# Layer A with keys-by-queries scores and a bounded exponential behind a runtime branch, and layer B's projections resident

## The chip, the cores and the metric

The kernel runs on one core of one Trainium2 chip. The metric is the device time of one execution in microseconds (us), median of several. The four executions of the kernel before lie within 0.24% (3440.38 to 3448.54). "Fast" is the label that the record gives to a run.

Five engines matter: PE (matrix products; PEld is its weight load), DVE (vector), ACT (scalar functions), POOL (general purpose) and SP (used here to issue DMA transfers). In the traces each has its own timeline, and for a wait the profile names what ended it, as in "PE b_tail <- DMA b_wq: 17.4 us" further down.

## The reference, cut to what matters

Four layers, A B A B, over 2048 tokens of width 640. Layer A has 32 heads of width 20. It works in four segments of 512 tokens. In each it computes causal softmax attention and, from the second segment on, a linear "memory" read; the two are mixed by a gate per head. phi(t) is t + 1 above 0 and exp(t) below. Layer B walks 64 steps in sequence (32 tokens plus 8 memory tokens each).

```python
x = x + _A_ref(_layernorm(x), A_wq, A_wk, A_wv, A_wo, A_beta)
x = x + _B_ref(_layernorm(x), B_mem0, B_Wq, B_Wk, B_Wv, B_Wo, B_seg_len)
# ... both once more

# inside _A_ref, for each of the 4 segments s:
logits = einsum('bhqd,bhkd->bhqk', qs, ks) * scale + mask   # mask: -1e9 above the diagonal
p      = softmax(logits);  a_dot = einsum('bhqk,bhkd->bhqd', p, vs)
a_mem  = einsum('bhld,bhde->bhle', phi(qs), M) / (phi(qs) . z + 1e-6)
o      = g * a_mem + (1 - g) * a_dot
M, z   = M + phi(ks)^T vs, z + sum(phi(ks))
```

The weights are drawn small. The product that the new kernel's bound tests is an estimated 0.0025 against a limit of 0.075, so these inputs take the bounded branch.

## The kernel before: the parts that the change touches

Layer A, one head of one segment (256 of these in the two layers), queries on the partitions:

```python
def S_stage(u):                       # scores, row maximum, exponential
    for qc in range(4):
        N = 128 * (qc + 1)
        nc.tensor.matmul(Sx[:, 0:N], lhsT=stt["qTm"][:, j, 128*qc:128*qc+128], rhs=kT[:, 0:N], ...)
        nc.tensor.matmul(Sx[:, N-128:N], lhsT=C.identb[:], rhs=C.negu[:], ...)      # causal mask, on PE
        nc.vector.tensor_reduce(out=negm[:], in_=Sx[:, 0:N], op=ALU.max, negate=True)
        nc.scalar.activation(out=Pj[:, OFFS[qc]:OFFS[qc]+N], in_=Sx[:, 0:N], func=ACT.Exp, bias=negm[:, 0:1])
def T_stage(u):                       # P has queries on partitions: transpose it for the value product
    for bi in range(8):
        nc.tensor.transpose(tpA[:, bi, :], Pj[...], C.identb[:])
    # ... 2 more into tpB; tpA and tpB copied to PTj by DVE and ACT
def PV_stage(u):
    nc.tensor.matmul(PVu[:, qc, :], lhsT=PTj[:, bidx, :], rhs=va[:, kc, j, :], ...)
```

The layer norm of the next segment is applied by DVE (`layernorm_tile`). The padded weights of A are built anew in each A layer, and all four weights of B (5.2 MB each) are loaded at each start of B:

```python
def load_B_weights(...):
    for nm, src in (("wq", B_Wq), ("wk", B_Wk), ("wv", B_Wv)):
        nc.sync.dma_start(t[:], src.rearrange("(c p) h e -> p c (h e)", p=128))
    nc.sync.dma_start(W.wo[:], B_Wo.rearrange("h e d -> e h d"))
```

## Time and profile before

| | us |
|---|---|
| median of 3 runs | 3443.7 (3440.38 to 3448.54) |
| span of the profiled run | 3445.3 |
| start, until the first score of A | 39.7 |
| A loop, first / second | 437.9 / 446.1 |
| tail of A (last score to last output projection) | 17.5 / 17.4 |
| joint (from there to the first step of B) | 61.5 / 62.6 |
| B and the second start of A | 1196.6 |
| second B | 1166.0 |

All such rows in this document are differences between the starts of first or last matmuls as the trace's tile view lists them (`a_S` scores, `a_YP` output projection, `b_Qa` first projection of a step of B), so that every kernel is cut at the same places.

The costliest groups of layer A (tiles: `a_S` scores, `a_negm` row maxima, `a_Pj` exponentials, `a_tpA` transposes), from the page of the kernel before (line, engine, operation, output<-input, shape, count, then busy us, mean ns of one, and what the idle time before it waited for):

```profile
L338 ACT ACTIVATE a_Pj<-a_S,a_negm 128x128 bf16<-128x128 f32 (+3 forms) x1024 | 504.0, 541 | 48.8 <-DVE a_negm L337 42.9
L337 DVE TENSOR_REDUCE a_negm<-a_S 128x1 f32<-128x128 f32 (+3 forms) x1024 | 467.7, 482 | 76.9 <-PE a_S L335 48.3
...
L348 PE MATMUL a_tpA<-c_identb,a_Pj 128*128 128x128 bf16 x2048 | 232.4, 220 | 8.0 <-ACT a_Pj L338 2.8
...
L335 PE MATMUL a_S<-c_negu,c_identb 128*128 128x128 bf16 x1024 | 221.3, 219 | 0.0
```

The two A loops in the windows view of the kernel before (stretch in us, its length, busy us of PE, PEld, DVE, ACT and POOL with their numbers of instructions, mean granted PE clock as a fraction of full speed, DMA share, GB/s):

```profile
40.00:478.00 438.00, 389.19 (x4968) 288.74 (x5008) 382.68 (x997) 375.96 (x857) 119.45 (x198) 0.99 0.09 27
1753.00:2199.00 446.00, 398.81 (x4967) 294.51 (x5003) 383.97 (x996) 377.60 (x857) 113.47 (x190) 0.97 0.10 30
```

In the loop PE is busy 389 of 438 us, DVE 383, ACT 376, and POOL only 119. Three engines are busy 86 to 89% of it at once, so the change sets out to relieve all three. At the joint the waits view shows PE waiting for B's weights (what waited, for what, us in all, times, longest):

```profile
PE b_tail L103 <- DMA b_wq<-in_B_Wq_dram: 17.4, 1, 17.4
PE b_tail L103 <- DMA b_wk<-in_B_Wk_dram: 6.1, 1, 6.1
...
PE b_tail L103 <- DMA b_wv<-in_B_Wv_dram: 5.2, 1, 5.2
```

### The profile page before, as it was taken

The page shows a single profiled execution, that of the slowest core. Times are in us where ns is not written, and L with a number is a line of the kernel's source. Part 1 is how long each engine was busy: PE and PEld are TensorE (multiplying, and loading weights), DVE is VectorE, ACT ScalarE, POOL GpSimd, SP SyncE. Part 2 cuts the span into 40 slices and gives each one's busy share as a digit, 9 for nine tenths or more (in the row PEclk, how much of TensorE's full clock was granted, in tenths as well). Part 3 has the DMA queues.
Part 4 walks back from the last instruction along what each step waited for, and adds up shares of the span by engine and source line. Part 5 has one row for each costly group of instructions (what it writes and reads, how often), then busy time and mean ns, then how long its engine had stood idle before and what let it go on. Part 6 is the DMA issues. An engine that isn't in the chain of part 4 may idle for free. (4 is left out here: it accounts for less than half of the span.)

```text
span 3445.3 us, 130756 instructions
## 1 busy us (share of the span) xinstructions
PE 3017.7 (88%) x56899; PEld 1780.5 (52%) x56980; DVE 2075.8 (60%) x5369; ACT 1691.9 (49%) x3987; POOL 660.2 (19%) x1687
## 2 busy tenths in 40 slices
PE   5988867999999999999769888679999999999998
PEld 4666643555454554555446666435555555554554
DVE  7888863555555555555488888625555555555554
ACT  5978852343333433334269788523443334333332
POOL 4242220111111111111132322201111111111111
PEclk9999987999999999999889999879999999999998
DMA  2010034000000000000120111340000000000000
GB/s 66 13 40 26 22 136 174 17 19 17 20 17 17 19 17 20 17 17 15 24 69 12 48 29 30 143 166 15 17 15 17 15 15 17 15 17 15 15 13 11
DMA packets 94208, 120.95 MB, mean 35 GB/s; under 512 B 31424, under 2 KB 79552, under 8 KB 89792
## 3 DMA queue, kind: packets, MB, share of 16 engines
q1 hardware_dynamic: 93632, 112.58, 10.9%
q8 instruction: 446, 7.31, 0.9%
q14 instruction: 130, 1.06, 0.1%
HBM read 72.13 MB, written 23.59 MB: 28 GB/s over the span
## 5 line engine op out<-in xcount | busy, mean ns | idle before, releaser
L103 PEld LDWEIGHTS <-b_hT 128*32 128x32 bf16 x15520 | 356.2, 96 | 376.9 <-DVE b_hT L103 46.6
L338 ACT ACTIVATE a_Pj<-a_S,a_negm 128x128 bf16<-128x128 f32 (+3 forms) x1024 | 504.0, 541 | 48.8 <-DVE a_negm L337 42.9
L337 DVE TENSOR_REDUCE a_negm<-a_S 128x1 f32<-128x128 f32 (+3 forms) x1024 | 467.7, 482 | 76.9 <-PE a_S L335 48.3
L103 PE MATMUL b_OPS<-b_wo,b_OTsb 128*32 128x320 bf16 x8192 | 318.5, 310 | 44.3 <-DVE b_OTsb L103 44.3
L103 PE MATMUL b_V<-b_wv,b_hT 128*32 128x512 bf16 x5120 | 346.9, 382 | 0.0
L103 POOL TENSOR_TENSOR b_P<-b_Pu,b_rs 128x256 bf16<-128x256 bf16 (+1 forms) x256 | 111.2, 455 | 1181.9 <-DVE b_rs L103 1181.9
L103 ACT ACTIVATE b_Pu<-b_SP 128x320 bf16<-128x320 f32 x256 | 111.9, 437 | 357.3 <-DVE b_SP L103 357.3
L103 PEld LDWEIGHTS <-b_OTsb 128*32 128x32 bf16 x8192 | 213.2, 100 | 118.4 <-DVE b_OTsb L103 57.9
L348 PE MATMUL a_tpA<-c_identb,a_Pj 128*128 128x128 bf16 x2048 | 232.4, 220 | 8.0 <-ACT a_Pj L338 2.8
L103 ACT COPY b_QT<-b_TPQ 128x128 bf16<-128x128 bf16 x508 | 178.3, 379 | 119.7 <-PE b_TPQ L103 115.9
L103 DVE COPY b_KT<-b_TPK 128x128 bf16<-128x128 bf16 x382 | 101.7, 266 | 218.6 <-PE b_TPK L103 218.6
L103 DVE CAST b_hT<-b_MT 128x24 bf16<-128x24 f32 x126 | 23.0, 183 | 330.7 <-PE b_MT L103 330.7
L335 PE MATMUL a_S<-c_negu,c_identb 128*128 128x128 bf16 x1024 | 221.3, 219 | 0.0
L103 ACT CAST b_msb<-b_OPS 128x320 bf16<-128x320 f32 x128 | 54.4, 425 | 296.3 <-PE b_OPS L103 296.3
L103 PE MATMUL b_Qa<-b_wq,b_hT 128*32 128x512 bf16 x2560 | 163.4, 384 | 34.7 <-DVE b_hT L103 34.7
L103 DVE CAST b_Ksb<-b_Ka 128x512 bf16<-128x512 f32 x128 | 88.5, 691 | 149.9 <-PE b_Ka L103 149.6
L103 ACT ACTIVATE b_Qsb<-b_Qb 128x512 bf16<-128x512 f32 x128 | 76.4, 597 | 198.1 <-PE b_Qb L103 198.1
L348 PEld LDWEIGHTS <-a_Pj 128*128 128x128 bf16 x2048 | 147.0, 98 | 50.2 <-issue 10.1
L103 PEld LDWEIGHTS <-b_hx 128*32 128x32 bf16 x3840 | 84.9, 98 | 164.7 <-issue 58.5
L103 DVE TENSOR_REDUCE b_negmax<-b_SP 128x8 f32<-128x320 f32 x256 | 124.8, 487 | 71.1 <-PE b_SP L103 71.1
L103 DVE TENSOR_REDUCE b_ssum<-b_Pu 128x8 f32<-128x320 bf16 x256 | 123.1, 481 | 72.4 <-ACT b_Pu L103 72.4
L103 DVE CAST b_Ksb<-b_Kb 128x512 bf16<-128x512 f32 x128 | 88.5, 691 | 125.9 <-PE b_Kb L103 125.9
(357 smaller groups left out, 6588.1 us busy)
## 6 DMA issues: line engine op xcount, KB each, us to landing
xres<-a_xnew SPq DMA_DIRECT2D x32, 320.0 KB
b_wq<-in_B_Wq_dram SPq DMA_DIRECT2D x2, 5120.0 KB
b_wk<-in_B_Wk_dram SPq DMA_DIRECT2D x2, 5120.0 KB
b_wv<-in_B_Wv_dram SPq DMA_DIRECT2D x2, 5120.0 KB
b_wo<-in_B_Wo_dram SPq DMA_DIRECT2D x2, 5120.0 KB
b_Vt<-b_Vtb SPq DMA_DIRECT2D x512, 16.0 KB
b_XO<-xres SPq DMA_DIRECT2D x256, 30.0 KB
xres_bf<-a_xnb SPq DMA_DIRECT2D x32, 160.0 KB
```

The lines of the kernel that those rows point to most:

```text
L103: r = f(*a, **k)
L335: nc.tensor.matmul(Sx[:, N - 128:N], lhsT=C.identb[:], rhs=C.negu[:], start=False, stop=True)
L337: nc.vector.tensor_reduce(out=negm[:], in_=Sx[:, 0:N], axis=AX.X, op=ALU.max, negate=True)
L338: nc.scalar.activation(out=Pj[:, OFFS[qc]:OFFS[qc] + N], in_=Sx[:, 0:N], func=ACT.Exp, bias=negm[:, 0:1], scale=1.0)
L348: nc.tensor.transpose(tpA[:, bi, :], Pj[:, OFFS[qc] + 128 * kc: OFFS[qc] + 128 * kc + 128], C.identb[:])
```

## The change

The intent: compute the scores with keys on the partitions, so that the exponential already has the layout which the value product needs. The transposes and their copies go away. A softmax without its row maximum is safe if |score| is bounded: the kernel computes a bound from the column norms of the weights at run time and branches. In the bounded branch the mask becomes a select on POOL after the exponential. Four heads of 32 padded rows are packed into PE's row tiles (the trace lists these matmuls as `32*128`, the full array's as `128*128`). B's wq, wk and wv are loaded once, during the first A layer, and stay; only wo is loaded at each B. The layer norm of the next segments moves from DVE to POOL.

The diff, cut to its core (cuts marked; the whole is 834 lines):

```diff
-def load_A_weights(nc, tc, ctx, C, A_wq, A_wk, A_wv, A_wo, A_beta):     # ... per A layer
+def prep_A(nc, tc, C, A_wq, A_wk, A_beta):                              # once
+        for k, src in enumerate((A_wq, A_wk)):
+            nc.gpsimd.memset(pad[:], 0.0)
+            # ... 5 copies into pad (3 DVE, 2 ACT), 8 stores of padded weights to DRAM
+            nc.gpsimd.tensor_tensor(out=sq[:], in0=raw[:], in1=raw[:], op=ALU.mult)
+            nc.vector.tensor_reduce(out=hs[:, k, :], in_=sq[:]..., op=ALU.add)
+        # ... maximum over heads, compared with the limit
+        W.bounded = nc.values_load(flag[0:1, 0:1])
 ...
+            def score(u, r):          # part r of unit u: two heads, one to three key blocks
+                for kc, c0 in ((0, 0),) if part == 0 else ((1, 0),) if part == 1 else ((2, 0), (3, 256)):
+                    for jj in range(2):
+                        nc.tensor.matmul(Sx[:, jj, c0:c0+N], lhsT=U.qk[32*j:32*j+32, 1, 128*kc:128*kc+128],
+                                         rhs=U.qk[32*j:32*j+32, 0, 128*kc:512], tile_position=(32*j, 0))
+                nc.scalar.activation(out=PT[:], in_=Sx[:, :, 0:N], func=ACT.Exp, scale=SC)
+                for c0 in ((0,), (0,), (0, 256))[part]:
+                    nc.gpsimd.affine_select(out=v, in_=v, pattern=[[0, 2], [1, 128]], compare_op=ALU.is_ge, fill=0.0, ...)
 ...
+                for slot in range(6):                       # one unit: 4 heads of one segment, 64 in all
+                    if u < NU: score(u, slot)
+                    if slot == 0 and more: proj(u + 1, 0)
+                    if slot == 1 and u >= 1: pvmm(u - 1, 1); norm(u - 1)
+                    if slot == 2 and more: proj(u + 1, 1); phi_q(u + 1)
+                    if slot == 4 and u < NU: pvmm(u, 0); # ... phi_k(u + 1)
+                    if slot == 5 and u < NU: nummm(u); memory(u)
+                    extras(u, slot)                         # output projection, layer norm, V projection
+        with tc.If(W.bounded > 0) as arm:
+            run(False, None)
+        with arm.Else(): # ... run(True, gctx): with row maximum
 ...
-                    WB = load_B_weights(nc, tc, bctx, B_Wq, B_Wk, B_Wv, B_Wo)
+        WB, loads = load_B_weights(nc, tc, ctx, B_Wq, B_Wk, B_Wv)      # at the start; issued within A's first loop
+                    nc.sync.dma_start(WB.wo[:], B_Wo.rearrange("h e d -> e h d"))
```

## The prediction

> What bounds the kernel now. The page spans 3445.3 us; the windows view places its stages. Layer A's head loop runs from 40 to 480 us and from 1753 to 2200 us; layer B runs from 557 to 1716 and from about 2280 to 3440 us, PE busy about 37 of every 40 us. B's code is unchanged, so its 2 x 1160 us stay.
>
> A's loop (13.75 us for four heads of one segment, 32 such units a layer) has no single limit: over 40:480 PE is busy 89%, DVE 87%, ACT 86%, POOL 27%. The groups (by form) show why: 512 row-maximum reductions (246 us of DVE), 512 exponentials with a per-row bias (277 us of ACT), 1280 transposes of P with their copies (about 143 us of DVE and ACT), and 512 mask matmuls. The change removes all of these in the bounded branch; these inputs satisfy the bound (estimated product 0.0025 against 0.075).
>
> Costs per unit after. ACT: two exponentials of 1024 and four of 768 elements, without bias. The trace has 128x320 without bias at 437 ns and 128x512 casts at 600, so 1024 takes about 1.03 us and 768 about 0.81: 5.3 us. With other exponentials and copies, 6.2 us in segment 0, 7.2 in 1 and 2, 6.4 in 3. [...]the biased form, interpolated to 320 elements, takes 543 ns. DVE: evictions (0.69 us each), phi, normalisation: 4.5 to 6 us. POOL takes over masking: eight selects of 256 elements (128 took 295 ns, so about 0.42 us each); with the rest about 6 us. PE: about 6 to 7 us.[...]
>
> So ACT is the floor, at about 218 us a layer, but [...]the score tiles have only two buffers. PV products wait for exponential and selects, the memory product for phi of K. I add about 1.5 to 2 us of bubbles a unit: 7.8, 9.3, 9.3 and 8.2 us in the four segments, 277 us a loop instead of 440. That saves about 163 us a layer, 326 in all.
>
> Joints. Resident B weights: before, A ends at 496.5 and B's first step starts at 556.6; PE waits about 17.5, 6.1 and 5.2 us for wq, wk and wv. But the serial prologue itself (tails, first projections, LN) is about 31 us, and afterwards its x load is queued behind the 5.2 MB of wo and starts only after the branch has joined. I expect 10 us saved at each joint. First head: before, the first score comes at 39.7 us; the bound, the padding round trip, LN, V projection and branch make it about 55 (+15). Second head: -4. Tails: -8; branches: +4.
>
> 3444 - 326 - 20 + 15 - 4 - 8 + 4 gives about 3105; I say 3095, range 3015 to 3180. Faster by over 2%: 0.97; within 2%: 0.02; slower: 0.01.
>
> The profile shows it right if A's loops take 250 to 300 us, ACT is busiest there (75 to 85%), PE idles before score and PV matmuls for ACT and POOL, B's steps are unchanged, and the A-to-B joint is 45 to 55 us. Wrong if: selects cost over 0.6 us (POOL sets the pace), row tiles do not overlap, the clock falls in A, the prefetch delays A's own loads, or joints shrink by 30 us or more.

## The result, and the profile after

| | before | after | difference | predicted |
|---|---|---|---|---|
| median, us (4 runs each) | 3443.39 | 3149.03 | -294.4 | 3095 (3015 to 3180) |
| start | 39.7 | 64.9 | +25.2 | +15 |
| two A loops | 437.9 + 446.1 | 285.0 + 286.5 | -312.5 | -326 |
| two tails | 17.5 + 17.4 | 14.7 + 16.6 | -3.6 | -8 |
| two joints | 61.5 + 62.6 | 59.1 + 61.2 | -3.8 | -20 |
| B and the second start | 1196.6 | 1195.0 | -1.6 | -4 |
| second B | 1166.0 | 1164.7 | -1.3 | 0 |
| span of the profiled run | 3445.3 | 3147.7 | -297.6 | |

The ratio is 0.9142, with a 95% interval of 0.9127 to 0.9158. A ratio here is the mean time of one kernel's fast runs over that of the other's fast runs of the same rounds, so it is not quite the ratio of the medians quoted.

The loops in the windows view of the changed kernel (columns as before):

```profile
65.00:350.00 285.00, 253.27 (x2704) 132.05 (x2732) 164.75 (x402) 198.26 (x269) 176.50 (x353) 0.92 0.42 136
1619.00:1905.00 286.00, 252.21 (x2702) 131.19 (x2732) 165.31 (x402) 198.31 (x269) 176.52 (x353) 0.93 0.32 99
```

PE is now busy 253 of 285 us (89%), ACT 198 (70%), POOL 176, DVE 165. The granted clock is lower than before: 0.92 and 0.93 in place of 0.99 and 0.97. PE, not ACT, is the busiest engine; what waits in its stream add is tested below. Groups of the first loop, by form, in the changed kernel follow. L84 is a helper through which it issues most instructions, so go by the tiles: `a_PP` query and key projections, `a_S` scores, `a_PT` exponentials, `a_pv` value products, `a_xn` the applied layer norm. On PE:

```profile
L84 PE MATMUL a_PP<-a_xnT_194,a_wt 128*128 128x512 bf16 x144 | 43.7, 422 | 2.0 <-issue 1.2
L84 PE MATMUL a_PP<-a_xnT_193,a_wt 128*128 128x512 bf16 x136 | 39.7, 405 | 2.0 <-DVE a_t1k L84 0.8 <-issue 0.4
L84 PE MATMUL a_S<-a_qk 32*128 32x512 bf16 x128 | 27.0, 418 | 0.3
...
```

on ACT:

```profile
L84 ACT ACTIVATE a_PT<-a_S 128x768 bf16<-128x768 f32 x127 | 101.7, 818 | 17.0 <-PE a_S L84 14.9 <-POOL a_PT L84 1.2
L84 ACT ACTIVATE a_PT<-a_S 128x1024 bf16<-128x1024 f32 x64 | 65.9, 1029 | 34.1 <-PE a_S L84 30.4 <-POOL a_PT L84 3.6
```

and on POOL:

```profile
L84 POOL TENSOR_SCALAR_AFFINE_SELECT a_PT<-a_PT 128x256 bf16<-128x256 bf16 x254 | 102.7, 425 | 86.9 <-ACT a_PT L84 85.8
L84 POOL TENSOR_SCALAR a_xn<-a_xt,a_mv,a_rstd 128x640 bf16<-128x640 bf16 x12 | 30.7, 2558 | 2.9 <-POOL a_rstd L84 2.2
```

The exponentials (0.82 and 1.03 us) and the selects (0.43 us) cost what had been predicted. The layer norm's application on POOL costs 2.56 us each. The waits view of the first loop shows whom PE waits for:

```profile
PEld L84 <- POOL a_PT L84: 27.9, 74, 1.5
...
PE a_pv L84 <- POOL a_PT L84: 13.3, 34, 1.2
```

So in this loop PE waits 13.3 us, and its weight loads 27.9 us (the two overlap: in these 285 us PE is busy 253 and PEld 132), for the selects that stand in front of the value products. ACT itself waits 45 us for PE's scores. One stretch in which PE waits for selects, in its timeline (start us, busy us, what, and in brackets the idle time before it and its releaser):

```profile
247.78 0.21 PE L84 MATMUL a_pv<-a_vaug_185,a_PT 128*128 128x21 bf16 x2 [0.41 <-POOL a_PT L84]
248.81 1.19 PE L84 MATMUL a_pv<-a_vaug_185,a_PT 128*128 128x21 bf16 x18 [0.82 <-POOL a_PT L84]
249.93 0.50 PE L84 MATMUL a_S<-a_qk 32*128 32x256 bf16 x4
250.36 2.31 PE L84 MATMUL a_PP<-a_xnT_193,a_wt 128*128 128x512 bf16 x5
```

POOL had a layer norm of 2.5 us in front of these selects, and PE waited 0.41 and 0.82 us for them. Right after it the five projection matmuls take 2.31 us; five of the same at 65.20 us, where the clock is at 1.00, take 1.25. The windows view of the same place shows the difference: the clock.

```profile
243.50:250.00 6.50, 4.31 (x52) 2.50 (x53) 2.14 (x7) 4.61 (x7) 5.66 (x9) 0.95 0.70 227
250.00:259.00 9.00, 8.78 (x63) 3.95 (x65) 5.48 (x15) 4.89 (x7) 5.85 (x10) 0.50 0.20 57
```

After a stretch in which PE was busy 4.31 of 6.5 us (66%), with no gap above 0.82 us, the clock is at 0.50 for 9 us. In slices of 0.5 us of the same view it is 1.00 up to 249.0 us, 0.50 from 249.5 to 259.5, and 1.00 again from 260.0.

The joint, in SP's and DVE's timelines of the changed kernel. First the issues:

```profile
373.46 0.39 SPq L1041 DMA_DIRECT2D b_wo<-in_B_Wo_dram  x1
374.03 9.31 SPq L617 DMA_DIRECT2D b_xt<-xres_bf  x1
```

then the first layer-norm statistic of B:

```profile
391.49 0.89 DVE L84 BATCH_NORM_STATS2 b_ln_st<-b_xt 128x6 f32<-128x320 bf16 x2 [16.90 <-DMA b_xt<-xres_bf]
```

The 5.2 MB of wo are issued first, x right behind it, and DVE waits 16.90 us for x.

### The profile page after: what moved, and what is told of

Read it like the earlier page. It is cut to its first block, busy times and chain, and to the rows that moved or that the text cites. A ratio compares the mean times of both kernels' runs of the same rounds, so it can differ in the third digit from the quotient of the medians.

```text
span 3147.7 us, 118684 instructions
## 1 busy us (share of the span) xinstructions
PE 2734.2 (87%) x52376; PEld 1461.4 (46%) x52438; DVE 1626.5 (52%) x4137; ACT 1328.7 (42%) x2798; POOL 756.3 (24%) x1975
## 5 line engine op out<-in xcount | busy, mean ns | idle before, releaser
L84 PEld LDWEIGHTS <-b_hT 128*32 128x32 bf16 x15520 | 355.5, 96 | 375.7 <-DVE b_hT L84 46.5
L84 POOL TENSOR_TENSOR b_P<-b_Pu,b_rs 128x256 bf16<-128x256 bf16 (+1 forms) x256 | 111.6, 457 | 1180.0 <-DVE b_rs L84 1172.7
L84 ACT ACTIVATE a_PT<-a_S 128x768 bf16<-128x768 f32 (+1 forms) x384 | 328.8, 888 | 103.8 <-PE a_S L84 91.4
L84 PE MATMUL b_OPS<-b_wo,b_OTsb 128*32 128x320 bf16 x8192 | 317.5, 310 | 44.7 <-DVE b_OTsb L84 44.7
L84 PE MATMUL b_V<-b_wv,b_hT 128*32 128x512 bf16 x5120 | 346.8, 382 | 0.0
L84 PEld LDWEIGHTS <-b_OTsb 128*32 128x32 bf16 x8192 | 212.8, 99 | 118.5 <-DVE b_OTsb L84 58.3
L84 ACT ACTIVATE b_Pu<-b_SP 128x320 bf16<-128x320 f32 x256 | 112.0, 437 | 357.0 <-DVE b_SP L84 357.0
L84 POOL TENSOR_SCALAR_AFFINE_SELECT a_PT<-a_PT 128x256 bf16<-128x256 bf16 x512 | 207.2, 425 | 175.6 <-ACT a_PT L84 173.3
L84 ACT COPY b_QT<-b_TPQ 128x128 bf16<-128x128 bf16 x508 | 178.2, 379 | 119.7 <-PE b_TPQ L84 115.9
L84 DVE COPY b_KT<-b_TPK 128x128 bf16<-128x128 bf16 x382 | 101.8, 267 | 217.9 <-PE b_TPK L84 217.9
L84 PE MATMUL b_Qa<-b_wq,b_hT 128*32 128x512 bf16 x2560 | 163.5, 384 | 34.7 <-DVE b_hT L84 34.7
L84 DVE CAST b_hT<-b_MT 128x24 bf16<-128x24 f32 x126 | 23.1, 183 | 329.6 <-PE b_MT L84 329.6
L84 ACT CAST b_msb<-b_OPS 128x320 bf16<-128x320 f32 x128 | 54.5, 426 | 296.1 <-PE b_OPS L84 296.1
L84 POOL COPY b_OTdef<-b_OTsb 128x256 bf16<-128x256 bf16 x128 | 51.0, 399 | 509.0 <-DVE b_OTsb L84 509.0
L84 DVE CAST b_Ksb<-b_Ka 128x512 bf16<-128x512 f32 x128 | 88.6, 692 | 149.0 <-PE b_Ka L84 148.8
L84 PE MATMUL b_Ka<-b_wk,b_hT 128*32 128x512 bf16 x2560 | 161.8, 382 | 0.0
L84 PE MATMUL b_Kb<-b_wk,b_hT 128*32 128x512 bf16 x2560 | 161.6, 381 | 0.0
L84 DVE TENSOR_REDUCE b_negmax<-b_SP 128x8 f32<-128x320 f32 x256 | 124.8, 487 | 71.1 <-PE b_SP L84 71.1
L84 DVE TENSOR_REDUCE b_ssum<-b_Pu 128x8 f32<-128x320 bf16 x256 | 123.2, 481 | 72.4 <-ACT b_Pu L84 72.4
L84 PE MATMUL b_Qb<-b_wq,b_hT 128*32 128x512 bf16 x2560 | 160.3, 379 | 0.0
L84 ACT ACTIVATE b_Qsb<-b_Qb 128x512 bf16<-128x512 f32 x128 | 76.4, 597 | 197.2 <-PE b_Qb L84 197.2
L84 DVE CAST b_Ksb<-b_Kb 128x512 bf16<-128x512 f32 x128 | 88.6, 692 | 125.8 <-PE b_Kb L84 125.8
```

What stands on the lines that cost most here:

```text
L84: r = f(*a, **k)
```

## The experiments

All are changes to the changed kernel ("after", 3149.0 us), unless said otherwise. All were checked against the reference and passed. The kernel before was run along with every batch: 3446.0, 3446.4, 3445.3 and 3444.5 us, so medians may be compared across batches to about 3 us.

### x before wo at the joint

```diff
-  nc.sync.dma_start(WB.wo[:], B_Wo.rearrange("h e d -> e h d"))                 # before layer_B
+  W.load_wo(nc.scalar)      # in layer_B, from ACT's queue, after the first layer norm's transpose
```

> B's first x load is issued before the 5.2 MB load of wo (which goes to ACT's queue after the first LN transpose). Theory Q (x waits behind wo): the wait from x's issue to the first LN statistic falls from 17.5 us to about 3, each A-to-B joint (last A output to first b_Qa) from 57 to about 43 us, total 3149 to about 3121. Rival J (the joint is the branch's join and the serial prologue): x still lands late or the prologue waits elsewhere, total within 5 us of 3149.

Measured: 3121.68 us (3118.68 to 3125.37), ratio to before 0.9057 [0.9042, 0.9073], 27.4 us less than after. The joints fall from 59.1 and 61.2 to 47.9 and 47.1 us; the loops together stay as they were (288.3 and 284.0). The mended start below gives the same two loop times, also with an unchanged loop; a loop difference of 3 us is thus no effect. DVE's timeline of this kernel, x having been issued at 376.46 us:

```profile
378.86 0.89 DVE L84 BATCH_NORM_STATS2 b_ln_st<-b_xt 128x6 f32<-128x320 bf16 x2 [1.31 <-DMA b_xt<-xres_bf]
```

The wait for x is 1.31 us in place of 16.90. The order of two transfers had cost 11 and 14 us at the two joints.

### Is it POOL's layer norm that holds up the selects?

First the one buffer of the normalised row (POOL must wait until PE has transposed the row before):

```diff
-            xn = wk1.tile([128, D], BF16, name="a_xn")     # one buffer
+            xn = wk.tile([128, D], BF16, name="a_xn")      # two
```

> The LN result tile a_xn gets two buffers instead of one; POOL still applies the LN. Theory W (POOL, [...]stands in front of the apply until PE has transposed the previous xn, and the mask selects queue behind it): units with an LN lose about 1.5 us, 16 of them matter, total about -25 us (3124). Rival D (only the length of the POOL op, 2.5 us, matters): less than 8 us. Rival P (those units are long because of V and output projections on PE): no change.

Measured: 3145.60 us (3142.70 to 3151.75), 0.9127 [0.9112, 0.9142]: 3.4 us less, loops 282.7 and 286.1. The theory fell.

Then the same, with the application itself on DVE:

```diff
-                            ln[tt] = ln_apply(nc.gpsimd, ln[tt], mv, rstd)
+                            ln[tt] = ln_apply(nc.vector, ln[tt], mv, rstd)
```

> Two buffers and the LN apply in the loop moved from POOL (2.5 us each, 12 a layer) to DVE (0.45 us). Theories W and D: units with an LN fall from 10.4-13 us to about 9, total about -40 us (3109), and the granted clock in the A loop rises from about 0.91 to 0.95. Rival P (PE work): total within 8 us of 3149.

Measured: 3167.66 us (3159.32 to 3172.75), 0.9186 [0.9167, 0.9204]: 18.6 us more, not 40 less. The operation is 4.9 times cheaper on DVE (512 ns in place of a median of 2508 ns on POOL), POOL's busy time falls to 147 us, and the loops grow to 294.6 and 297.2 us:

```profile
65.00:359.00 294.00, 256.69 (x2695) 132.49 (x2724) 170.80 (x414) 197.94 (x269) 147.49 (x340) 0.89 0.40 132
1632.00:1929.00 297.00, 256.69 (x2704) 133.03 (x2734) 173.69 (x414) 197.80 (x269) 149.70 (x341) 0.89 0.31 95
```

The clock column is the one to look at: 0.89. Multiply each loop by its clock for an estimate of the time it would take at full speed, if PE alone paced it: 285.0 x 0.92 = 262 us for after, 294.6 x 0.89 = 262 us here. By this estimate the whole difference lies in the clock. Why it falls further here is not settled: DVE now waits for POOL's reciprocal root (8.0 us in twelve waits in the first loop) with PE's evictions behind it in its stream, which would open other holes, but no run isolates that.

### The selects left out

```diff
-                for c0 in ((0,), (0,), (0, 256))[part]:
-                    nc.gpsimd.affine_select(out=v, in_=v, ...)
```

This kernel is wrong: it lets keys from the future into the diagonal blocks. (The tolerance of the comparison still let it pass, probably since layer A adds little to x with these weights.)

> The mask selects on POOL are left out (WRONG RESULT ON PURPOSE). If the selects pace the A loop, it falls from 288 us to 250 or less, total to about 3070. If PE and ACT pace it, and PE only stops now and then for a select (14 us a layer by the waits), it falls to 265-275 us, total about 3110 to 3125.

Measured: 3091.69 us (3091.37 to 3095.97), 0.8977 [0.8962, 0.8992], 57 us less. Between the two expectations. The loops in the windows view:

```profile
65.00:318.00 253.00, 230.39 (x2700) 125.25 (x2728) 162.54 (x402) 195.16 (x269) 76.79 (x99) 0.99 0.46 153
1591.00:1848.00 257.00, 234.74 (x2706) 126.75 (x2738) 162.64 (x402) 195.23 (x269) 76.80 (x99) 0.96 0.36 110
```

253.4 and 256.7 us, with the clock back at 0.99 and 0.96. By the same estimate that is 251 and 246 us at full speed against 262 and 266: so of some 30 us a loop, 11 to 20 are missing waits and the rest is the clock. The reading: the selects make PE wait, and the holes in its stream also lower its clock. This kernel alone does not prove the second half; the next two try it.

### Dummy matmuls into the holes, twice

```diff
+                if "spare" in wts and not general:
+                    for i_ in range(8):          # columns 384:512 of a score bank, which nothing reads
+                        nc.tensor.matmul(sp[:, i_ % 2, 384:512], lhsT=C.identb[:], rhs=C.identb[:], ...)
```

> Bounded branch only: eight dummy 128x128 matmuls, into columns of a score bank that nothing reads, before each of the two value products of a unit (64 units, so 1024 more matmuls, about 0.85 us of PE work a unit). Theory C (the granted clock falls in layer A because PE's stream has short holes while it waits for POOL's selects and ACT's exponentials; work in those holes would hold the clock): [...]the loop from 288 us to 268-273 us, the total to about 3112 us. Rival F (the dips do not come from the holes, and PE's own work paces the loop): each filler is added to the time, 0.85 us x 64 = up to 54 us, so 3175 to 3200 us.

Measured: 3384.07 us (3378.82 to 3391.71), 0.9816 [0.9796, 0.9836], far above both expectations. The waits view of the first loop of this kernel says why:

```profile
PE a_S L84 <- ACT a_PT L84: 90.9, 64, 2.1
```

The bank (a score tile, `a_S`) was the one which ACT was still reading, so the batches of dummies waited for the exponential. Once it ran, the batch at 244.64 us took 0.44 us (244.64 to 245.08 in PE's timeline), 0.88 for the two of a unit, where 0.85 had been expected. The run measures a mistake in the experiment, not the question. It was mended by writing columns 21 to 31 of the value bank, which nothing reads and whose release the value product has to await in any case:

```diff
+                for i_ in range(0 if general else 8):
+                    h = 2 * (i_ % 2)
+                    nc.tensor.matmul(pv[:, 0, h:h+2, :, 21:32], lhsT=C.identb[:], rhs=C.identb[:, 0:88], ...)
```

> Mended form of e4_fill, which had made a new wait (the dummy matmuls wrote the bank that ACT was still reading, PE waited 182 us for it). Now eight dummy matmuls of 88 columns go into columns of the value bank that nothing reads, right before each of the two value products; they wait for nothing that the value product itself does not wait for. By the trace's own short matmuls (four of 84 columns in 0.33 us) they are 0.4 to 0.7 us of PE work each time, 26 to 45 us in all. Theory C (holes in PE's stream let the clock fall): the filler falls into the holes, the mean clock of the loops rises from 0.92 to 0.96 or more, the loops shorten from 285 to 270-278 us, total 3120 to 3140 us. Rival F (PE's own work paces the loops, the clock falls for another reason): clock stays within 0.02 of 0.92 or falls, each loop grows by 10 to 22 us, total 3170 to 3195 us.

Measured: 3153.57 us (3148.07 to 3155.51), 0.9156 [0.9141, 0.9171]: the same as after within the spread. The loops:

```profile
65.00:351.00 286.00, 266.31 (x3236) 151.47 (x3235) 164.12 (x402) 199.55 (x269) 177.41 (x353) 0.96 0.41 136
1624.00:1908.00 284.00, 264.21 (x3225) 150.98 (x3224) 164.62 (x402) 199.67 (x269) 176.71 (x352) 0.96 0.32 100
```

286.3 and 284.6 us as in after, but at a clock of 0.96. The half of theory C that is shown: with more work for PE in these places and nothing else changed, the clock rose from 0.92 and 0.93 to 0.96. The dummies run in front of the waits and do not fill them. At the place shown above PE still waits 0.82 us for a select, but it was busy 4.87 us of the 6.5 instead of 4.31, and the clock stays full there; the five projections right after it take 1.25 us:

```profile
243.50:250.00 6.50, 4.87 (x62) 2.89 (x61) 2.17 (x7) 4.55 (x7) 5.80 (x10) 1.00 0.72 224
250.00:259.00 9.00, 7.99 (x78) 4.16 (x74) 5.57 (x15) 5.30 (x7) 6.80 (x11) 0.81 0.19 58
```

In this pair the same longest hole, 0.82 us, goes with both clocks; what differs is how busy PE was over the short stretch, 66% in front of the 0.50 and 75% here. The share of the whole loop does not decide: it was 89% in the kernel before too, at 0.99. Nor do the row tiles: the kernel without selects has them and ran at 0.99 and 0.96. The theory's hope, a faster loop, fell: by the estimate above it is now 275 us at full speed in place of 262, so the dummies cost what the clock gave. The filler was no cure here; the next run takes waits away instead.

### The value products one slot later

The same work, but the selects get one slot more before PE needs their result.

```diff
-                    if slot == 1 and u >= 1:
+                    if slot == 2 and u >= 1:
                         pvmm(u - 1, 1); norm(u - 1)
-                    if slot == 4 and u < NU: pvmm(u, 0)
+                    if slot == 5 and u < NU: pvmm(u, 0)
```

> The two value products of a unit are placed one slot later (second one of the unit before from slot 1 to 2, first one from slot 4 to 5), so that every select and exponential has one slot (about 1.4 us) more before PE needs it; the work is the same. Theory S (what e3_nosel gained, 57 us, is the select's latency in front of the value products, which holds up PE and lets the clock fall): 40 to 57 us less than the changed kernel, 3092 to 3110 us, loops 262 to 268 us[...]. Rival P (PE's own work and the score-bank handshake with ACT pace the loop, latency of selects does not): at most 10 us less, 3139 to 3149 us.

Measured: 3126.35 us (3124.56 to 3128.01), 0.9069 [0.9054, 0.9084], 22.7 us less: between the theories. The loops fall to 277.0 us each, at 0.93 and 0.94. In the waits view of the first loop the selects have nearly gone from PE's list:

```profile
PEld L84 <- POOL a_PT L84: 6.8, 26, 1.3
PE a_S L84 <- ACT a_PT L84: 6.5, 16, 0.9
```

PE's weight loads wait 6.8 us for selects in place of 27.9, and PE's own wait of 13.3 us is down to 1.9 us; scores now wait 6.5 us for their banks (3.1 before). The latency of the selects is thus worth 8 to 10 us a loop by itself; it is not the whole of what leaving them out gained. The clock rose by only 0.01, though these waits were nearly gone, so they alone do not account for the lower clock.

### The selects on DVE

This starts from the combination described last and replaces the select by a product with a 0/1 triangle on DVE, one slot after the exponential.

```diff
-                    nc.gpsimd.affine_select(out=v, in_=v, ...)
+                    sel.append(lambda v=v: nc.vector.tensor_tensor(out=v, in0=v, in1=tri..., op=ALU.mult))
```

> e8_best with one more change: in the bounded branch the causal selects are a multiplication by a 0/1 triangle on DVE, put one slot after the exponential, in place of the selects on POOL. POOL loses 207 us of its work; DVE gains 512 operations of 256 bf16 elements, estimated from its own copies at 0.2 to 0.35 us, 50 to 90 us a loop on top of 165. Theory V (POOL's load and its queue cost the loops their clock and some stalls; without selects 57 us were gained): loops from about 277 to 262-268 us at a clock of 0.95 or more, total 20 to 30 us less than e8_best. Rival D (DVE's evictions of the projections are on PE's chain, 43 us of DVE waiting for PE and back, so more DVE work delays PE as much as POOL did; the layer norm put on DVE cost 19 us): equal to e8_best within 8 us or slower by up to 30 us.

Measured: 3141.84 us (3125.23 to 3149.68), 0.9114 [0.9080, 0.9147]: 54 us more than the combination. The product takes 291 ns against 415 for the select, POOL's busy time falls to 77 us, and the loops grow from 275.0 and 277.3 to 306.9 and 299.6 us:

```profile
52.00:359.00 307.00, 261.04 (x2714) 134.69 (x2715) 213.29 (x652) 195.04 (x268) 77.03 (x98) 0.88 0.38 127
1609.00:1908.00 299.00, 252.91 (x2710) 131.46 (x2709) 213.45 (x651) 195.11 (x268) 77.03 (x98) 0.91 0.30 94
```

DVE is busy only 70% of the loop, and its masks hardly ever waited for an exponential (1.3 us in the first loop), but PE's weight loads waited 19.5 us for masks. That the 63 us of masks a loop delay the evictions queued behind them on DVE is likely, not shown. What is shown is that POOL's load by itself is not what costs the clock: it was 77 us here, as without selects. Rival D's direction held, its size (up to 30) was too small. With the layer norm's move above, this is the second time that taking work off POOL and giving it to DVE lost time, at a lower clock (0.88 and 0.91).

### The residency alone undone

```diff
-        WB, loads = load_B_weights(nc, tc, ctx, B_Wq, B_Wk, B_Wv)        # resident, prefetched in A
+                    WB, loads = load_B_weights(nc, tc, bctx, B_Wq, B_Wk, B_Wv)   # per B layer
+                    for f in loads: f()
```

> The residency alone is undone: wq, wk and wv of B are loaded again at each start of B (15 transfers, 15.7 MB) and nothing is prefetched in layer A; all else is the changed kernel. Theory Q (the joint between A and B is held by the order output weights, x, layer norm, first projections behind the runtime branch, so the loads that residency saves mostly ran beside that chain): each joint grows from 57 us to 62-70 us, the first A loop gains 0-5 us as its first segment loses the prefetch; total +10 to +25, 3159 to 3175 us. Rival R (residency takes away all three weight waits that the kernel before showed, 17.4 + 6.1 + 5.2 = 29 us a joint): total +50 to +60, about 3200 to 3210 us.

Measured: 3189.28 us (3185.15 to 3193.72), 0.9256 [0.9241, 0.9272], 40 us more; neither expectation. The sum of it: start +9.9 us (74.8), first loop +2.8, joints +12.1 and +12.1 (71.2 and 73.3). The start explains what had been overlooked: the scheduler had moved the load of wo to the very start of the program, ahead of A's weights, which cost 10 us there and at the same time took wo away from the joint. Two things had changed. So the last run undid the residency on top of the first experiment, in which wo is bound to its place behind x:

> e1_xfirst (x before the output weights) with residency undone as in e6_reload. In e6_reload the compiler's scheduler had moved the load of the output weights to the very start, so that run changed two things. Here the output weights are loaded after x again. Theory Q2 (residency is worth more once x is not queued behind the output weights: in e6_reload PE waited 13.1 + 4.6 + 5.4 us for the three weights in the first joint): joints of 68 to 75 us in place of 47.9 and 47.1, start back at 64-66 us, total +40 to +55 over e1_xfirst, 3160 to 3177 us. Rival (residency is worth the 12 us a joint that e6_reload showed against the changed kernel): joints of about 60 us, total about 3146 us.

Measured: 3196.45 us (3189.52 to 3199.79), 0.9283 [0.9268, 0.9299], 74.8 us more than with x first and resident weights. The start is 65.2 us again, the joints 88.4 and 85.8 us. Both expectations were too low. The waits view of the first joint in this kernel:

```profile
PE b_tail L84 <- DMA b_wq<-in_B_Wq_dram: 17.8, 5, 8.5
...
PE b_tail L84 <- DMA b_wk<-in_B_Wk_dram: 16.4, 3, 12.6
...
PE b_tail L84 <- DMA b_wv<-in_B_Wv_dram: 5.9, 3, 3.2
```

PE waits 17.8 + 16.4 + 5.9 = 40 us, about the difference of the first joint (88.4 - 47.9 = 40.5). But this run, too, mixes two things. It issues wo from ACT's queue just before the three weights, 0.37 us ahead of the first of them:

```profile
381.71 0.39 ACTq L84 DMA_DIRECT2D b_wo<-in_B_Wo_dram  x1
382.08 2.58 SPq L547 DMA_DIRECT2D b_wq<-in_B_Wq_dram  x5
```

In the previous run (residency alone undone, wo at the program's start) the same three loads made a joint of 71.2 us, also with x in front of them. Residency alone is thus worth 71.2 - 47.9 = 23 us, and the other 17 us come with wo's load beside the three. Now the first joint can be taken apart:

| first joint | us |
|---|---|
| before: all four weights loaded there (wo last), x loaded while A ends | 61.5 |
| branch, x first, three weights loaded there, wo at the program's start | 71.2 |
| branch, x first, all four weights loaded there (wo first) | 88.4 |
| branch, x first, three resident, wo after x | 47.9 |
| branch, wo before x, three resident (the changed kernel) | 59.1 |

In the kernel before, x's load and its layer norm lay inside A's tail (the first statistic of B's layer norm ran at 486.6 us, A's end was at about 495), and so did the wait for them. Behind the runtime branch x was issued only after A's end (374.0 us in the changed kernel, A's last output projection 364.6); what does not depend on A could still move ahead of the branch, as wo did. From the first row to the second are 10 us: the branch with the order of loads that goes with it. Residency takes away 23 us, wo in front of x puts 11 us back, and 2.4 us remain.

### The start

```diff
-            nc.gpsimd.memset(pad[:], 0.0)                     # one in front of each square
+            # both memsets first
-            nc.gpsimd.tensor_tensor(out=sq[:], in0=raw[:], in1=raw[:], op=ALU.mult)
+            nc.scalar.activation(out=sq[:], in_=raw[:], func=ACT.Square)
-            ln_apply((nc_raw.vector, nc_raw.gpsimd)[tt % 2], xt, mv, rstd)
+            ln_apply(nc_raw.vector, xt, mv, rstd)
```

> Only the start is changed: the two squares of the bound go from POOL to ACT, both pad memsets go first on POOL, and the first segment's layer norm is applied on DVE alone. Theory H (the start is long because POOL's squares, 5.5 us each, run in series with its 4.4 us memsets and at the same time hold up DVE's copies, 15.8 us for three against 0.8 us for the same three with POOL idle; the branch then waits for the flag): the flag comes at 20-24 us instead of 32.7, the first score at 50-56 us instead of 64.9, and the second start loses 2-4 us with it through the layer norm; total -10 to -18, 3131 to 3139 us. Rival L (the start is bound by DMA: weights in, padded weights out and in again, x after the branch): first score at 61 us or later, total -4 or less.

Measured: 3133.14 us (3129.75 to 3142.20), 0.9098 [0.9081, 0.9115], 15.9 us less. The first score comes at 53.2 us in place of 64.9, the flag's last operation at 19.4 us in place of 32.6. Theory H holds; the flag comes 13.2 us earlier, more than the 11.7 us gained, so the layer norm's move to DVE, which the run does not separate, is not needed to explain it. In the changed kernel POOL runs like this (its timeline; start us, busy us):

```profile
8.09 5.52 POOL L139 TENSOR_TENSOR a_sq_115<-a_raw_98 128x3200 f32<-128x3200 bf16 x1 [2.57 <-DMA a_raw_98<-in_A_wq_dram]
13.55 4.37 POOL L128 MEMSET a_pad_120<- 128x5120 bf16 x1
17.87 5.59 POOL L139 TENSOR_TENSOR a_sq_135<-a_raw_118 128x3200 f32<-128x3200 bf16 x1
```

and DVE:

```profile
8.11 15.77 DVE L135 COPY a_pad_100<-a_raw_98 128x640 bf16<-128x640 bf16 x3 [1.96 <-DMA a_raw_98<-in_A_wq_dram]
...
27.33 0.78 DVE L135 COPY a_pad_120<-a_raw_118 128x640 bf16<-128x640 bf16 x3
```

Three copies of the same shape take 15.77 us while POOL works and 0.78 us when it has finished. In the mended kernel, DVE's timeline:

```profile
5.81 4.08 DVE L161 TENSOR_SCALAR a_gg<-a_gg 128x32 f32<-128x32 f32 x1
8.04 2.49 DVE L138 COPY a_pad<-a_raw 128x640 bf16<-128x640 bf16 x3
...
19.52 0.80 DVE L138 COPY a_pad<-a_raw 128x640 bf16<-128x640 bf16 x3
```

This DVE operation of 32 columns (`a_gg`) took 0.18 us in the changed kernel, with POOL idle; here it shows 4.08 us and ends at 9.89, just after the second memset on POOL ends at 9.86 us. Of the three copies that take 15.77 us, one ends at 18.09, just after POOL's memset (17.92), the next at 23.64, just after its square (23.46), and the third takes 0.32 us with POOL idle. In both traces a slow DVE operation thus ends within 0.2 us of one on POOL; by what mechanism, no run here shows. In the A loop little of it can be seen: leaving out POOL's selects lowered DVE's busy time there only from 164.8 to 162.5 us.

### The combination

x first, value products one slot later, and the mended start.

> The three edits that each gained are put together: x before the output weights at the joint (-27.4 us alone), the start with squares on ACT and layer norm on DVE (-16.0 us alone), value products one slot later (-22.7 us alone). If they add up, as they lie in different stages (joints, starts, loops): 3149.0 - 66.1 = 3083 us, and it should lie in 3075 to 3095 us. If the clock of the loops or the joints takes part of it back: 3095 to 3110 us.

Measured: 3087.86 us (3086.11 to 3089.80), 0.8964 [0.8949, 0.8979]. The three gains add up within 5 us (3083 expected). Start 53.4, loops 275.0 and 277.3, joints 47.5 and 43.0 us. It is 61 us faster than the changed kernel and beats both; its result is correct, unlike that of the kernel without selects, which it equals in time.

## Why the prediction was right or wrong

The total was within the range, 54 us (1.7%) slower than the point. The sum of the prediction's own terms was 3105, and it then stepped 10 us below it for no stated reason; that step was in the wrong direction. (Its +4 us for the branches has no row of its own in the table.)

- **The removal.** Right: the row maxima, biased exponentials, transposes, their copies and the mask matmuls were gone, and the loops fell to 285.0 and 286.5 us against 277 predicted (-312.5 us against -326).
- **What sets the loop's pace.** Wrong, though the number was near. "ACT is the floor, at about 218 us a layer" and "busiest there (75 to 85%)": ACT was busy 198 us a layer, 70%. "PE: about 6 to 7 us" a unit was the term that failed: PE was busy 253 us over 32 units, 7.9 us each, 89% of the loop. Part of this is work that was under-counted and part is the clock (with the clock at 0.99 and no selects PE was busy 230 us, 7.2 us a unit). The bubbles that were added to ACT's floor stood in by chance for PE's stream.
- **The bubbles' cause.** Half right: PE did wait in front of value products for POOL's selects (13.3 us, and 27.9 us of weight loads, in the first loop), hardly in front of scores (3.1 us). "The clock falls in A" was listed as a risk, and it happened: 0.92 and 0.93. In the filler pair it went with how busy PE was over a short stretch (66% of 6.5 us in front of 0.50, 75% at 1.00); which holes in PE's stream weigh most, no run separates.
- **Costs of single operations.** Right where a duration in the trace stood behind them: select 425 ns (0.42), exponentials 818 and 1029 ns (0.81 and 1.03). The prediction's reading that an exponential without a per-row bias is cheaper (437 ns against 543 at 320 elements) held with them: by an estimate from the line through 818 and 1029 ns, 512 elements take 607 ns without the bias, where 512 with it took 699 ns before. Not costed was the layer norm on POOL: a median of 2.51 us.
- **Row tiles.** They overlap in part. In PE's timeline at the first unit, a pair of 512-column score matmuls in two row tiles starts at 64.88 and the next group at 65.20, 0.32 us later; five full-array matmuls of 512 columns take from 65.20 to 66.39, 0.24 us each. Two in turn would be 0.48 us. Why the pair takes 0.32 us and not less, no run here shows.
- **Joints.** The mechanism was predicted (x queued behind wo, no start before the branch has joined), the size was not: -3.8 us for both in place of -20, and 59.1 and 61.2 us where its own check said 45 to 55. The runs show that residency is worth 23 us at the first joint and that the branch (10) and wo in front of x (11) take back 21 of them.
- **Start.** +25.2 us in place of +15. The missing part was POOL's serial 20 us of memsets and squares, and DVE's copies beside them (15.77 us in place of 0.78); mending it gave 11.7 us back.
- **B.** Right: unchanged, the last stretch within 1.3 us.

What stays open: why the clock falls further when work moves from POOL to DVE; how busy PE has to be to keep its clock; and how the remaining gain of leaving out the selects (20 to 24 us a loop beyond what one slot more brings) divides between POOL's queue and the clock.

## What to carry to other kernels

When a change moves the limit from several engines to PE, count PE's stream a unit at a time and look at the granted clock: at the place shown here, waits of 0.41 and 0.82 us in front of PE were followed by 10 us at a clock of 0.50. Making a resident copy or removing a wait pays only if what stands behind it can start (at the first joint here, 21 of the 23 us of residency were taken back): look at what a runtime branch forbids to start early, and at which transfer is first in the queue. Place small, latency-critical transfers ahead of big ones (27.4 us less here), and give a result that crosses two engines one pipeline slot more (22.7 us less); here neither cost anything.
